# Sigmoid attention and token mixer on one core: order of steps planned anew, all output in 64x64 tiles, exchange and casts on VectorE

## The chip, the core and the metric

The kernel runs on one core of one Trainium2 chip. The metric is the device time of one execution in microseconds (us), lower is better; a kernel's time is the median of its runs. The profile is one further execution; its span counts from the first to the last instruction.

## What is computed

```python
# q, k, v: (8, 12, 448, 64) float32; moe_w_q, moe_w_k: (768, 64); moe_w_out: (768, 768)
scores = q @ k.T / sqrt(64) - log(448)
x = sigmoid(scores) @ v                        # per batch and head
x = x.transpose(0, 2, 1, 3).reshape(8, 448, 768)
wq, wk = x @ moe_w_q, x @ moe_w_k              # (8, 448, 64)
mixed = (wq @ wk.T / sqrt(64)) @ x             # per batch
out = relu(mixed) @ moe_w_out                  # (8, 448, 768)
```

The kernel never forms `wq @ wk.T`: it computes `wk.T @ x` (64 by 768 per batch) and multiplies `wq` with that.

## The kernel before

**Tiling.** Four heads of one batch make a group ("quad" in the code): 24 groups, three to a batch. 448 rows are 64 partitions times 7, so a group's attention is seven steps. A score step (`scores`) is four matmuls of 64x64 tiles, one for each quarter of TensorE, that fill a pair of PSUM banks; one ACT instruction takes the sigmoid of the pair, 128x896, to bf16. A value step (`values`) is four more 64x64 matmuls, which accumulate over the seven steps in another pair of banks; after the seventh, the pair is evicted to `xt`, on DVE as a rule. There are 168 score steps and 168 value steps.

**From the inputs to a group.** Loads are issued on the SP queue into a ring of eight 448 KB buffers (`pump_loads`, order in `ORDER`). Each load of q, k or v is cast to bf16 by POOL, unless `ORDER` marks it: with a dot for DVE, as a capital for ACT (`cast_next`). q and k must then be transposed. Four ways exist, chosen for each group by a letter of the plan:
- "a"/"b" and "q"/"k": transposes on TensorE, in 128x128 or 64x64 blocks, and an eviction from PSUM by DVE;
- "c"/"d": POOL exchanges quadrants of 32 partitions with six copies 32x448 (`arrange`, over the scratch tile `swap`), then DVE transposes 32x32 blocks in two instructions for each of q and k;
- "r"/"s"/"z": no exchange; DVE transposes straight to the exchanged quadrants, two instructions of 128x448 ("r") and four of 32x448 ("s" and "z").

**After a batch's three groups.** `tr_x` transposes `xt` ("X" in 128x128 blocks, "x" in 64x64), `mlp_wqk` makes wq and wk ("W" in 128x128, "w", "l" in 64x64), `mlp_wkn` transposes wk, `mlp_tmp` ("U", "T") makes `wk.T @ x`, `mlp_mix` ("M", "m") multiplies with wq and takes the relu, and the letters "O", "o", "Q", "I", "i" are parts of the output product. For batches in pair `TW` (pairs 1 and 2 of 0 to 3) mixing and output use 64x64 tiles: an output tile is four parts of twelve matmuls in one pair of banks (`out_pair`), and `mlp_mix` writes 256-column halves. For pairs 0 and 3 the output is made in 128x128 tiles of 384 columns (`out_chunk`) or in 64x64 tiles with a sum on DVE (`out_halves`). 64x64 output needs the rows of w_out a second time with the partition halves exchanged: the letter "C" copies one block of `wout16` with two DMAs on SP, six letters in all. w_out itself is loaded and cast by two DMAs from POOL's queue (`load_wout`, when POOL comes to the entries w1 and w4 of `ORDER`).

**What sets the order.** Nothing is scheduled by a library. `PLAN` is a string of 639 letters, worked off from left to right by the last loop; each letter issues one step. An engine's instructions run in the order in which they were issued, and TensorE waits where a step waits. "S" is a score step with its sigmoid, "P", "p", "R" a value step, "1" the next cast of DVE's list, "2" the next of ACT's, "F" a matmul of zeros. `BANKS` names, for every step that opens a PSUM result, the bank or pair of banks (eight in all); a bank is written again when its readers are done. POOL's casts are issued as early as `ready` allows: two buffers each for casted q and k, four for v. From the 45th load on (`LATE`), two loads are let go for each finished output tile, and stand behind that tile's stores on SP.

Score steps are counted below from 0 to 167: group n begins with step 7n.

## Time and profile before

| | |
|---|---|
| median of 3 runs | 183.79 us (182.34 to 184.23) |
| span of the profiled execution | 180.4 us |
| PE, matmuls | busy 170.3 us, 94% of the span |
| ACT | busy 159.0 us, 88% |
| DVE | busy 143.7 us, 80% |
| POOL | busy 122.9 us, 68% |
| DMA | 47.29 MB, mean 262 GB/s |

PE is TensorE's matmuls, PEld its weight loads, DVE VectorE, ACT ScalarE, POOL GpSimd, SP the engine that issues most DMAs. A row of a group gives line, engine, operation, out<-in, shapes and count, then busy us and the mean ns of one, then the idle time in front of them and what ended it. Matmuls overlap, so the mean of one is longer than the time by which it moves the next one on. The share of an engine's busy time is a mean over stretches with different limits, and has to be read stretch by stretch.

### The profile page before, as it was taken

To read this page: it belongs to the slowest core of one execution; us is meant where nothing else is said; L and a number is where in the kernel's file an instruction comes from. 1 tells how busy PE (TensorE), PEld (TensorE's weight loads), DVE (VectorE), ACT (ScalarE), POOL (GpSimd) and SP (SyncE) were. 2 spreads that over 40 slices of the span, in tenths; PEclk is the share of its full clock that TensorE was granted. 3 is DMA by queue.
4 is the path that set the end of the run, shared out by engine and by line. 5 is a ranking of instruction groups with operands and counts; after the bars stand their busy time and mean duration, and the time that the engine had idled before them with its cause. 6 is when DMAs were issued, how large, how long until landed. Compare 5 with 4: busy or idle time off the path is not lost.

```text
span 180.4 us, 7849 instructions
## 1 busy us (share of the span) xinstructions
PE 170.3 (94%) x3412; PEld 114.1 (63%) x3412; DVE 143.7 (80%) x226; ACT 159.0 (88%) x208; POOL 122.9 (68%) x167
## 2 busy tenths in 40 slices
PE   7898899889999999999999999999999999999990
PEld 7444445444675555546667786677888888888660
DVE  3566899998988896989999999978789885868351
ACT  4599999999999999999999999998999989976310
POOL 1076899798999999999999999889978810010000
PEclk9999999999999999999999999999999999999999
DMA  5999999999999989699997999968596432505876
GB/s 169 353 394 346 325 385 376 283 304 366 339 305 358 349 266 299 226 318 349 279 318 277 257 307 329 372 215 272 137 336 166 131 88 48 137 4 123 207 196 174
DMA packets 24914, 47.29 MB, mean 262 GB/s; under 512 B 3888, under 2 KB 18480, under 8 KB 24880
## 3 DMA queue, kind: packets, MB, share of 16 engines
q1 hardware_dynamic: 23600, 44.64, 76.8%
q0 software_dynamic: 800, 1.18, 3.6%
q10 hardware_dynamic: 480, 0.98, 1.5%
q8 instruction: 26, 0.43, 0.9%
q14 instruction: 8, 0.07, 0.1%
HBM read 35.78 MB, written 11.01 MB: 259 GB/s over the span
## 4 chain that ended last, share of the span: by engine, by line
PE 61%; DMA 16%; ACT 7%; POOL 5%; DVE 4%; SPq 3%; issue 2%; POOLq 0%
PE banks L530 15%; PE banks L341 11%; PE banks L319 11%; PE banks L611 9%; DMA k<-in_k_dram 8%; ACT at L324 7%; DMA v<-in_v_dram 5%; DMA w<-in_moe_w_k_dram 4%; PE banks L570 3%; POOL qk L192 2%; PE banks L404 2%; PE banks L416 2%; PE banks L379 2%; PE banks L363 2%; PE banks L484 1%
## 5 line engine op out<-in xcount | busy, mean ns | idle before, releaser
L324 ACT ACTIVATE at<-banks 128x896 bf16<-128x896 f32 x168 | 139.8, 951 | 2.9 <-PE banks L319 2.4
L319 PE MATMUL banks<-qk 64*64 64x448 bf16 x672 | 62.0, 357 | 3.3 <-ACT at L324 2.0
L341 PE MATMUL banks<-at,v 64*64 64x448 bf16 x672 | 47.3, 351 | 0.8 <-ACT at L324 0.7
L319 PEld LDWEIGHTS <-qk 64*64 64x64 bf16 x672 | 25.7, 105 | 21.5 <-issue 13.3
L530 PE MATMUL banks<-wout,mx 64*64 64x384 bf16 x672 | 36.2, 323 | 0.0
L192 POOL CAST qk<-k 128x896 bf16<-128x896 f32 x19 | 22.7, 1196 | 10.1 <-DMA k<-in_k_dram 9.7
L341 PEld LDWEIGHTS <-v 64*64 64x64 bf16 x672 | 23.2, 106 | 8.4 <-issue 1.8
L350 DVE CAST xt<-banks 128x896 bf16<-128x896 f32 x22 | 23.8, 1084 | 2.5 <-PE banks L341 2.0
L530 PEld LDWEIGHTS <-mx 64*64 64x64 bf16 x672 | 22.6, 107 | 4.5 <-issue 0.2
L611 PE MATMUL banks<-wout,mx 128*128 128x384 bf16 (+1 forms) x138 | 24.4, 320 | 0.0
L192 POOL CAST qk<-q 128x896 bf16<-128x896 f32 x18 | 21.5, 1193 | 2.5 <-DVE qk L276 1.0
L471 DVE TENSOR_SCALAR mx<-banks 128x1024 bf16<-128x1024 f32 (+3 forms) x22 | 21.3, 970 | 1.9 <-PE banks L484 0.7
L209 POOL CAST v<-v 128x896 bf16<-128x896 f32 x22 | 20.6, 952 | 1.8 <-DMA v<-in_v_dram 1.3
L611 PEld LDWEIGHTS <-mx 128*128 128x128 bf16 x138 | 12.3, 98 | 9.8 <-issue 3.2
L167 POOL COPY qk<-swap 32x448 uint32<-32x448 uint32 x28 | 16.3, 584 | 1.6
L276 DVE STREAM_TRANSPOSE qk<-qk 128x448 f32<-128x448 f32 x28 | 17.0, 628 | 0.5 <-POOL qk L164 0.4
L161 POOL COPY swap<-qk 32x448 uint32<-32x448 uint32 x28 | 15.6, 556 | 2.5 <-DVE qk L192 0.8
L164 POOL COPY qk<-qk 32x448 uint32<-32x448 uint32 x28 | 15.6, 555 | 1.6
L245 DVE STREAM_TRANSPOSE qk<-qk 32x448 f32<-32x448 f32 x24 | 15.3, 636 | 0.6
L413 POOL COPY wq<-wqk 64x448 bf16<-64x448 bf16 x3 | 1.7, 556 | 15.8 <-DVE wqk L412 15.8
L644 DVE COPY o<-banks 128x384 f32<-128x384 f32 x12 | 6.6, 553 | 5.7 <-PE banks L611 5.3
L392 DVE COPY xn<-banks 128x1024 bf16<-128x1024 bf16 (+1 forms) x14 | 8.8, 625 | 2.8 <-PE banks L379 2.7
(89 smaller groups left out, 203.8 us busy)
## 6 DMA issues: line engine op xcount, KB each, us to landing
q<-in_q_dram SPq DMA_DIRECT2D x24, 448.0 KB, 6.3
v<-in_v_dram SPq DMA_DIRECT2D x24, 448.0 KB, 6.0
k<-in_k_dram SPq DMA_DIRECT2D x23, 448.0 KB, 6.9
out_dram<-o SPq DMA_DIRECT2D x50, 192.0 KB, 4.2
wout<-in_moe_w_out_dram POOLq DMA_DIRECT2D x2, 576.0 KB, 11.6
wout<-wout SPq DMA_DIRECT2D x12, 96.0 KB, 6.4
out_dram<-o ACTq DMA_DIRECT2D x4, 192.0 KB, 3.2
k<-in_k_dram SPq DMA_DIRECT2D x1, 256.0 KB, 4.8
```

Of the source, the lines that this page charges most:

```text
L161: eng.tensor_copy(out=z[lo], in_=w[hi, 0])
L167: eng.tensor_copy(out=w[lo, 1], in_=z[lo])
L192: COPY[e](out=f[:, :, "qk".index(nm)].rearrange("p e i d y -> p e y i d"), in_=ld.pop((nm, n)).rearrange("p (y i e d) -> p e y i d", y=2, ...
L209: COPY[e](out=t16.rearrange("p b i d -> p (b i d)"), in_=ld.pop((nm, n)).rearrange("p b x -> p (b x)"),)
L276: nc.vector.transpose(out=qk[n][:, t].rearrange("p t i n -> p (t i n)").bitcast(F32), in_=w)
L319: nc.tensor.matmul(sc[HALF[h], g, 0:S], qk[n][HALF[g], h, 1, i, :], qk[n][HALF[g], h, 0].rearrange("p i n -> p (i n)"), start=True, stop=True,
L324: inst = nc.scalar.activation(at, sc[:, :, 0:S], ACTF.Sigmoid, bias=attn_bias, scale=attn_scale)
L341: nc.tensor.matmul(ps[HALF[g], h, 0:S], ld["v16", n][HALF[h], g, i, :], ats[n, i][HALF[h], g, :], start=(i == 0), stop=(i == NI - 1),)
L350: read(fb, COPY[eng](out=xt(u, j)[:, :, 0:S], in_=ps[:, :, 0:S]))
L471: inst = nc.vector.tensor_scalar(dst, ps, moe_scale, 0.0, ALU.mult, ALU.max)
L530: nc.tensor.matmul(ps[HALF[x], y, 0:NB], mx[HALF[y], u, b, 64 * (i - 3 * y) : 64 * (i - 3 * y) + 64], wout16[HALF[y], slot(y, b), x * NB : ...
L611: nc.tensor.matmul(ps, mxs[w][:, 2 * S * c + m * P : 2 * S * c + (m + 1) * P], wout16[:, c, w0:w1], start=(c == 0), stop=(c == NC - 1),)
```

## The change

`PLAN`, `BANKS` and `ORDER` are replaced as a whole. By the letters and the instructions that come of them:
- All four pairs of batches are in `TW`: the output is made by `out_pair` alone (28 tiles), mixing in 256-column halves; `out_chunk` and `out_halves` are not used.
- Groups 1, 2, 3 and 6 are transposed on TensorE in 64x64 blocks ("q"/"k"; before: group 1 in 128x128, groups 3 and 6 in 64x64). Groups 4 and 5 have the new letter "v": loads and casts as for "c", but the six exchange copies are issued on DVE, at the place of the letter, in front of the transposes. All other groups, 7 to 23, are exchanged on POOL (17 groups, 14 before). The way "r"/"s"/"z" (six groups before) is not used.
- 21 casts stand on DVE (k1, q1 to q4, k6, q12, k13, k18, q18 and eleven of v; six before), none on ACT (before: one of v and three entries of w).
- `tr_x` uses 128x128 blocks 3 times instead of 10; five matmuls of zeros instead of ten.
- The copies "C" stand together while batch 0 is mixed, between score steps 29 and 36; on SP, one stands behind the load of q8 and the other five, ten DMAs, behind that of k9. Before they stood between steps 35 and 84.
- `LATE` is 46 instead of 44.

```diff
--- before.py
+++ after.py
@@ -65,17 +65,17 @@
     banks16 = banks.rearrange("p b x -> p (b x)").bitcast(BF16).rearrange("p (b x) -> p b x", b=8)
 
     BANKS = (
-        "01 23 45 7 7 67 01 23 5 5 45 67 45 1 01 23 67 5 5 45 3 23 1 01 67 5 45 23 01 67 45 01 45 "
...
+        "01 23 45 7 7 67 01 23 5 5 45 67 01 4 45 23 67 01 23 45 67 01 23 45 67 23 45 01 23 67 45 "
+        "01 45 67 01 45 67 01 45 23 0 45 67 1 23 45 0 67 23 45 1 67 01 45 2 67 01 23 45 67 01 23 "
+        "45 67 23 01 67 23 01 67 23 45 6 23 7 45 01 23 45 23 01 67 45 6 01 67 4 01 23 45 67 23 "
...
     )
     BANKS = BANKS.split()[::-1]
 
@@ -126,23 +126,23 @@
         return xts[u % 2 * NJ + j]
 
 
-    TW = (1, 2,)
+    TW = (0, 1, 2, 3, )
 
 
     PLAN = (
-        "FFSSSFFKSSF11aSSbFFrSFSFSSFSqSPPsPPSPzkPSPSPPPSxSrSsPPPPSPPS"
-        "PSPPPPSSXWzSSwWWSWWXSNSSPPPrSsPPUSPPzSPSPSPCMPPPSPSqkSSMSXSM"
-        "SCcPPPSPPxSPdPSOSwwrSSwwWWxSOSSOsOSNPPSPPzCPSPPSIISISIcPSPdP"
-        "PSPS2SPPOOSxSUSPPSMPPPcSPPSdOwWwSSMWWWoSMPPSPPPP1SSPcdOQSxSO"
-        "OSSNCSOOXcdSSOOSTSPPPSrPPCPSPPCPPSPPPSPSOwowSSSwsOzOxSwwWPSP"
-        "MSPPPPRSScSdXXOXoSMSOoNSMPPSPcPPSPPSUdSOSMOSOMoPSPPcPPSPSdPw"
-        "WXWSMSWWWXSSONOScTSOSOSOOdSPOSrOSPPPGPPSPPPSPPsPSPOSPOSOzSQS"
-        "XPcPPSPPPSPOSOdSOSxOlLlSLlLPSPPPxPP2GSPOOScOmdOSOOSNO1SQSTPP"
-        "PcS1PPSPOPSOSOQSMOSOSOdScOOSdOMSOmOP2PSPPxSPPP12SOSOSOSxOllL"
-        "SllcSLPPPSPPPSPOOdSxSOOSOSOSONQSTPSPPPSPPPSPPPxPPmPPLxLlMlGL"
-        "lOOyOoNIItIiIMimIiMOoOOOoOoOOOOOOOOOoOO"
+        "FFSSSFFKSSF1S11qSkS1SSqPP1RkpSpSRPqSkSSRRRSx1SSvPPSRdSSPPpRp"
+        "RSPPSSXSSWWWSvWWSWXSdPPpCPPSPNPSS1SCUqkSCSCCSMMCSPSpRSMPSpPS"
+        "PRSPPRS1cRSRPWWWSXSSWxWWSdPRSxRcRSPRNSPSUSxSMRdpSpSMSPppPSoS"
+        "OSQcSOOdSoSGoOSoS1QxSOS1OSPRSRpcPdpPSPRpSpxSRPPSQS1oxSOScdOS"
+        "OOS1oSOS1PPPRSpPPlSlllcdSllSOOS1QOSRPSRPpNSpPcdSOoSOSxQtSxSw"
+        "wwwwwGRpSPRNGPRGRSTocdSoSOQSxoSO1SMcOSOpPRSPmRPPQSoSdMQSORPS"
+        "RxpSRPPSQcSQxdSOSO1S1pPpRRSORSoSPQSOSoQcdSxSQ1OcSLLLSLLLSPPR"
+        "SppPPSoSOSdxOSOpSppRSpRNPSwUScSxwwwwwpGpSNppdPGGRuSPQSQSMQSQ"
+        "QcdSQSxOGOS1QSOMSQSOSPpPRScP1doSoRSPOSOSPRpPSPpPcSQSQxSQSdOL"
+        "1SLLLLSLSQocSoSOPSPRPdSPNpPSOSQxSQQSpTSPRSppPPSRPpmPPPplmllm"
+        "lllyyoOxNoOQtOooMQmOMoQOoooOoOOoooOOQOQ"
     )
-    KIND = ["a"] + [t for t in PLAN if t in "qacer"]
+    KIND = ["a"] + [t for t in PLAN if t in "qacerv"]
 
     ld = {}
     SRC = dict(q=q, k=k, v=v)
@@ -152,7 +152,7 @@
     def arrange(n, eng):
 
         arranged.add(n)
-        if KIND[n] in "er":
+        if KIND[n] in "r":
             return
         w = pq[n].rearrange("p e t i d y -> p e (t i d y)").bitcast(U32)
         z = p_one.tile([P, 2 * NI * 32], U32, tag="swap", name="swap")
@@ -168,7 +168,7 @@
 
     def load1(n, nm, eng):
         u, j = quads[n]
-        if KIND[n] in "cer" and nm != "v":
+        if KIND[n] in "crv" and nm != "v":
             t = p_ld.tile([P, 2 * NI * HD], F32, tag="ld", name=nm + "32")
             eng.dma_start(
                 out=t, in_=SRC[nm][u, 4 * j : 4 * j + 4].rearrange("h (p r) d -> (h p) (r d)", r=2 * NI),
@@ -185,7 +185,7 @@
         ld[nm, n] = t
 
     def cast1(n, nm, e):
-        if KIND[n] in "cer" and nm != "v":
+        if KIND[n] in "crv" and nm != "v":
             if n not in pq:
                 pq[n] = p_c16.tile([P, 2, 2, NI, 32, 2], BF16, tag="qk16", name="qk16")
             f = pq[n]
@@ -195,7 +195,10 @@
             )
             ld[nm + "16", n] = f
             if ("q16", n) in ld and ("k16", n) in ld:
-                arrange(n, nc.gpsimd)
+                if KIND[n] == "v":
+                    arranged.add(n)
+                else:
+                    arrange(n, nc.gpsimd)
             return
         if nm == "v":
             t16 = p_v16.tile([P, 2, NI, HD], BF16, tag="v16", name="v16")
@@ -268,7 +271,9 @@
             for e in range(2):
                 nc.vector.transpose(out=qk[n][:, e].rearrange("p t i n -> p (t i n)").bitcast(F32), in_=w[:, e])
             return
-        if kind in "cdef":
+        if kind == "v":
+            arrange(n, nc.vector)
+        if kind in "cdefv":
             assert n in arranged
             w = pq[n].rearrange("p e t i d y -> p e (t i d y)").bitcast(F32)[:, t]
             if t == 0:
@@ -694,10 +699,10 @@
 
 
     ORDER = (
-        ".q1 .k1 k2 q2 q3 v0 w2 k3 v1 k4 q4 v2 w0 k5 q5 w1 v3 W5 v4 q6 k6 w4 k7 v5 q7 v6 q8 k8 k9 "
-        "q9 v7 q10 v8 k10 v9 k11 q11 k12 k13 v10 .q12 q13 v11 v12 v13 q14 k14 k15 q15 v14 q16 k16 "
-        "v15 q17 k17 k18 q18 q19 v16 v17 v18 k19 V19 W3 q20 .q22 q21 k20 W6 k21 .k22 v20 q23 k23 "
-        "v21 .v22 v23 "
+        ".k1 .q1 .q2 k2 .v0 .q3 k3 v1 k4 .q4 v2 k5 w0 q5 q6 v3 .k6 v4 v5 w1 .v6 k7 w4 k8 q7 q8 "
+        "v7 q9 k9 q10 k10 .v8 .v9 .q12 k11 q11 .v10 k12 q13 .k13 .v11 v12 k14 q14 q15 k15 .v13 "
+        "v14 k16 q16 v15 k17 q17 .k18 .q18 v17 .v16 q19 k19 v18 q20 k20 k21 q21 .v19 q22 .v20 "
+        "k22 k23 q23 .v21 v22 v23 "
     )
     BY = {"s": [], "v": []}
     for x in ORDER.split():
@@ -711,7 +716,7 @@
     done = dict.fromkeys("SPqkKxWNUMOCgz", 0)
     used, loaded, cast = set(), set(), set()
 
-    LATE = 44
+    LATE = 46
     ring = [("q", 0), ("k", 0)]
 
     allowed = [2]
@@ -812,7 +817,7 @@
     used |= {("q", 0), ("k", 0)}
     pump()
 
-    ALIKE = dict(a="q", c="q", e="q", r="q", b="k", d="k", f="k", s="k", j="k", h="k", X="x", y="x", Y="x", g="g", z="z", L="W", l="W", T="U", t="U", I="O", i="O", Q="O", G="M", R="P")
+    ALIKE = dict(v="q", a="q", c="q", e="q", r="q", b="k", d="k", f="k", s="k", j="k", h="k", X="x", y="x", Y="x", g="g", z="z", L="W", l="W", T="U", t="U", I="O", i="O", Q="O", G="M", R="P")
     done["q"] = done["k"] = 1
     quads_r = []
 
@@ -843,7 +848,7 @@
             tr(c, kind, t)
             if t in "df":
                 used.add(("q", c))
-            if t not in "cers":
+            if t not in "cersv":
                 used.add((kind, c))
                 pump()
         elif t == "g":
```

18 rows, old and new, of the table BANKS are left out of this document.

## Prediction

> **What bounds the kernel now.** I read the page's head first, then the busy time in stretches, cut where the sigmoids reach a certain number, then the chain of waits. The head has the span:
>
> ```profile
> span 180.4 us, 7849 instructions
> ```
>
> The median of the three runs is 183.79 us, 3.4 more than this span; I add 3.4 to a span to get a time. The next view gives busy us and number of instructions for PE, PEld, DVE, ACT and POOL in each stretch, then clock, DMA share and GB/s:
>
> ```profile
> 0.00:7.00 7.00, 6.01 (x56) 4.79 (x56) 3.05 (x16) 2.51 (x5) 0.70 (x6) 1.00 0.72 222
> 7.00:58.20 51.20, 47.06 (x892) 25.86 (x888) 44.03 (x67) 51.20 (x63) 42.31 (x53) 1.00 1.05 345
> 58.20:90.20 32.00, 31.91 (x512) 17.88 (x508) 27.77 (x42) 31.18 (x42) 30.19 (x41) 1.00 0.91 299
> 90.20:155.60 65.40, 64.77 (x1578) 50.45 (x1571) 55.53 (x78) 63.38 (x81) 49.12 (x68) 1.00 0.74 231
> 155.60:176.00 20.40, 20.40 (x400) 15.13 (x392) 12.79 (x25) 10.69 (x22) 0.56 (x1) 1.00 0.51 129
> ```
>
> Three regimes. From 7 to 58 us ACT is busy 51.20 of 51.20: sigmoids set the pace, and PE is not full. From 58 to 155.6 us PE (31.91 of 32.00, 64.77 of 65.40) and ACT are both full. After that PE alone works. The sigmoids themselves, in the same stretch and over the run:
>
> ```profile
> 7.00:58.20 51.20, 51.20 (x63) 1.00 1.05 345
> ```
> ```profile
> L324 ACT ACTIVATE at<-banks x168: 911/934/1086, 7.0 to 155.6; 128x896 bf16<-128x896 f32 x168
> ```
>
> So one sigmoid costs 51.20/63 = 0.81 us, and in the first regime sigmoid number k (from 0) is due at 7.0 + 0.81k. I write S23 for number 23, which belongs to group 3 (7 a group). The last one starts at 155.6, and the last eviction stands in the chain at
>
> ```profile
> 176.20 0.36 DVE o L633
> ```
>
> which leaves 4.2 us for it and the last store.
>
> **PE's work.** The chain of waits has start and length of each block, start to start where PE is the bound:
>
> ```profile
> 86.89 0.45 PE banks L363 x8
> 87.33 0.49 PE banks L611 x3
> 87.82 0.31 PE banks L319 x4
> 88.13 0.22 PE banks L484 x8
> 88.35 0.19 PE banks L319 x4
> ...
> 94.30 0.49 PE banks L530 x12
> ```
>
> Three 128x128 matmuls (L611) and twelve 64x64 ones (L530) do the same share of the output in the same 0.49 us: 64x64 tiles neither cost nor save streaming. Four score matmuls take 0.19 us behind 64x64 work but 0.31 behind L611: a change of tile shape costs up to 0.12 us. In the order of instructions there are 68 such changes before and 34 after. Those before S63 (35 and 25) lie in the stretch where ACT is the bound. Between S63 and S98 they go from 22 to 2, behind that from 11 to 7.
>
> Transposes of x in eight 128x128 blocks (L363) take 0.45 us. The 64x64 form, by starts in the timeline,
>
> ```profile
> 45.02 0.45 PE L379 MATMUL banks<-ident,xt 64*64 64x64 bf16 x32
> 45.30 0.36 PE L319 MATMUL banks<-qk 64*64 64x448 bf16 x4
> ```
>
> takes 0.28. The wide form goes from 10 to 3 uses. Mixing in 256-column halves is eight matmuls in 0.22 (L484), where the form for batches 0, 1, 6 and 7 had four of 448 columns, 0.19 like the scores: 12 times 0.03, nothing.
>
> I add up each stretch's matmuls by their columns at 448 in 0.19 us (quarter tiles four at a time), and the tile changes at 0.12. S63 to S98: before 27.9 + 2.6 = 30.5 of the 32.0 us, after 31.4 + 0.2 = 31.6, since output steps have been moved forward into this stretch: +1.1. S98 to the last sigmoid: before 63.5 + 1.2 = 64.7 of 65.4, after 61.3 + 0.8 = 62.1: -2.6. After the last sigmoid: 20.5 (for the 20.40) against 18.7: -1.8.
>
> **ACT and the evictions.** These groups carry the prices that follow (busy us, mean ns):
>
> ```profile
> L350 DVE CAST xt<-banks 128x896 bf16<-128x896 f32 x22 | 23.8, 1084 | 2.5 <-PE banks L341 2.0
> ...
> L192 POOL CAST qk<-q 128x896 bf16<-128x896 f32 x18 | 21.5, 1193 | 2.5 <-DVE qk L276 1.0 <-DMA q<-in_q_dram 0.9 <-POOL qk L167 0.4
> ...
> L276 DVE STREAM_TRANSPOSE qk<-qk 128x448 f32<-128x448 f32 x28 | 17.0, 628 | 0.5 <-POOL qk L164 0.4
> ...
> L161 POOL COPY swap<-qk 32x448 uint32<-32x448 uint32 x28 | 15.6, 556 | 2.5 <-DVE qk L192 0.8
> ...
> L541 DVE COPY o<-banks 128x384 f32<-128x384 f32 x4 | 2.2, 557 | 1.2 <-PE banks L530 0.9 <-issue 0.3
> ...
> L469 ACT ACTIVATE mx<-banks 128x512 bf16<-128x512 f32 x2 | 1.2, 600 | 0.5 <-PE banks L484 0.5
> ...
> L788 DVE CAST k<-k 128x512 bf16<-128x512 f32 x1 | 0.4, 427 | 0.4 <-DMA k<-in_k_dram 0.4
> ...
> L788 DVE CAST k<-k 128x384 bf16<-128x384 f32 x1 | 0.4, 360 | 0.1
> ```
>
> ACT gets eight half relus (L469, 0.60) before its last sigmoid instead of two and loses about as many output copies and a cast: I count +1. It falls between S63 and the end of the sigmoids, where PE's work becomes less; with PE, ACT and DVE then all within some per cent of full, I take +0.7 (0 to +1.5). The last store is 192 KB a DMA instead of 96, its eviction 0.56 (L541) instead of 0.36. Median us to landing:
>
> ```profile
> k<-in_k_dram SPq DMA_DIRECT2D x23, 448.0 KB, 6.9
> out_dram<-o SPq DMA_DIRECT2D x50, 192.0 KB, 4.2
> wout<-in_moe_w_out_dram POOLq DMA_DIRECT2D x2, 576.0 KB, 11.6
> ...
> out_dram<-o SPq DMA_DIRECT2D x2, 96.0 KB, 2.5
> ```
>
> That would be +1.9; the 4.2 comes from busier stretches, so I take +0.7.
>
> Without new waits: 180.4 + 1.1 - 2.6 - 1.8 + 0.7 + 0.7 = 178.5, a time of 181.9.
>
> **The new waits.** After the change 21 casts (6 before, 4 of them after the start) and 12 exchange copies run on DVE. None of it is on PE, but DVE takes its work in order, and the evictions that free PSUM banks stand behind. What DVE and POOL do to each other is in the timeline (start, length):
>
> ```profile
> 64.48 1.58 POOL L167 COPY qk<-swap 32x448 uint32<-32x448 uint32 x2
> ...
> 126.56 1.17 POOL L164 COPY qk<-qk 32x448 uint32<-32x448 uint32 x2
> ```
> ```profile
> 64.98 0.68 DVE L192 CAST qk<-q 128x896 bf16<-128x896 f32 x1
> ```
> ```profile
> 142.25 1.06 DVE L209 CAST v<-v 128x896 bf16<-128x896 f32 x1
> ```
> ```profile
> 141.90 2.20 POOL L209 CAST v<-v 128x896 bf16<-128x896 f32 x2
> ```
>
> Two POOL copies take 1.17 us alone and 1.58 when a DVE cast from SBUF to SBUF starts between them: POOL pays 0.4. At 142 us a cast on DVE takes 1.06 instead of some 0.65 because a POOL cast is under way, and the POOL pair takes 2.20. Each holds the other up. [...]
>
> The place where it matters is group 4. Its exchange ("v" in the plan) stands on DVE behind S17, so from about 20.8 us. Behind it stand both transposes of group 4 and then the eviction of group 1's values, whose bank pair is the one S23 writes; S23 is due at 7.0 + 23 x 0.81 = 25.7. A DVE copy of 448 words lies between the two L788 rows: 0.39. Without waits: 20.8 + 6 x 0.39 + 2 x 0.63 + 1.08 = 25.5, just in time. But POOL's timeline there, with nearly the same casts after the change, is
>
> ```profile
> 20.59 0.94 POOL L209 CAST v<-v 128x896 bf16<-128x896 f32 x1
> 22.10 2.18 POOL L760 CAST wqk<-w 64x384 bf16<-64x384 f32 x4 [0.57 <-DMA w<-in_moe_w_k_dram]
> 24.35 1.19 POOL L192 CAST qk<-k 128x896 bf16<-128x896 f32 x1
> 25.44 1.19 POOL L192 CAST qk<-q 128x896 bf16<-128x896 f32 x1
> ```
>
> If each copy waits for one of these: 0.94 + 4 x 0.55 + 1.19 = 4.3 more, and S23 is 4.1 late. Group 5's exchange, behind S26, holds up the eviction of batch 0's wqk, for which PE waits ahead of S30: 0 to 1.2. ACT has no other work there, so this is lost. I take 3.0 of the 0 to 5.3, about half, as POOL also waits for loads.
>
> Late, POOL is the engine with little room: it exchanges 17 groups instead of 14 (six copies of 0.56), and 15 casts on DVE that meet it cost 0.4 each, 6 us. Loads for group 22 are queued on SP behind a store at S137, 17 steps ahead of S154. At 65.4/70 = 0.93 a step that is 15.9 us. They need 6.9 to land, two casts (2.4), the exchange (3.3) and two transposes (1.3), 13.9, and SP waits for the evictions of the stores in front:
>
> ```profile
> SPq L551 <- DVE o L543: 13.2, 4, 4.5
> ```
>
> 13.2 us in 4 waits. I take 1.5 (0 to 4) for this and group 23.
>
> The sum: 178.5 + 3.0 + 1.5 = 183.0, a time of **186.4 us**.
>
> **Rivals.** *The waits do not come* (the copies slip between POOL's instructions, POOL keeps its lead): 181.9, and down to 179.7 where the levelled engines cost nothing, the store lands as now and half of the 1.5 us that PE's sum leaves free between S63 and S98 goes too. It decides at group 4: exchange and transposes done by 24.5, S23 is not late. For it: 25.5 against 25.7 fits, and PE's savings lie where PE is 99% busy. Against it: four rows that show the hold-up.
>
> *The weight copies block the loads.* The twelve copies of wout ("C") stand on SP directly behind the loads up to group 8 and 9, ten in a row. The first waits for POOL's casting DMA, 11.6 us to landing, which POOL issues near 32: SP stands until about 43. v7, q9 and k9 are behind it: landed by 50, casts and exchange 5.7, transposes 1.3: 57, against S63 due at 58.2. One us of room; with the exchanges' hold-ups and ten more issues ahead of q10 and k10 up to 4 us go: 187 to 190. Against it: SP idle lets the weights land sooner.
>
> *The change is neutral*: half of the waits, 183 to 185.5; speaks for it that each wait was priced at half of a wide range.
>
> **Chances.** Under 1% (1.8 us here) I call no change. Forecast, slower by waits on DVE and POOL: 0.42. SP blocked by the weight copies, slower: 0.09. No waits: 0.34, of which 0.07 ends within 1%. Neutral: 0.15. So faster 0.27, same 0.22, slower 0.51. The range: low end 179.7 (the first rival), high end 191.0 (5.3 and 2.7 for the waits instead of 3.0 and 1.5, and the store's 1.9), together 8 in 10.
>
> **What would show it.** Right: six exchange copies on DVE near 21 us that last over 4 us together with gaps to POOL's instructions; a wait of ACT for scores of 1 us or more between 24 and 33; the sigmoids from S63 to the last in about 98 us (97.4 before); PE after the last sigmoid 18.7. POOL copy pairs of 1.6 instead of 1.17 where DVE casts. Wrong: S63 at 58 us (then the waits were nothing), or ACT waiting for PE in 60 to 155 where I see PE relieved, or SP's wait for wout as the longest.

## The result and the profile after

| | median us | runs |
|---|---|---|
| before | 183.06 | 181.49 to 184.23 |
| after | 198.43 | 195.25 to 200.86 |
| ratio | 1.080 | 95% interval 1.064 to 1.096 |

The change costs 8%, where 186.4 us (179.7 to 191.0) were predicted. The ratio is of the faster executions of each kernel, and the profiled execution of the kernel after, 200.86 us, is the slowest of its four.

The head of the page after, then one row of the page before:

```profile
span 199.0 us, 9232 instructions
...
PE 172.2 (87%) x4122; PEld 123.7 (62%) x4123; DVE 146.6 (74%) x216; ACT 160.5 (81%) x207; POOL 121.0 (61%) x169
...
PEclk9996889987999999999879999999999999999998
...
q8 instruction: 32, 0.52, 1.1%
```
```profile
q8 instruction: 26, 0.43, 0.9%
```

PE is less busy (87%, 94% before), it has 1421 instructions more, its clock dips four times, and queue q8 fetches 32 packets, each of 16,384 bytes, instead of 26. The stretches below are cut at the starts of S0, S35, S63, S98 and of the last sigmoid (columns as in the prediction: busy us of PE, PEld, DVE, ACT, POOL, then clock, DMA share, GB/s). Before, the rows that the prediction did not need:

```profile
7.00:35.30 28.30, 25.10 (x432) 12.77 (x425) 23.00 (x36) 28.30 (x36) 21.41 (x24) 1.00 1.05 356
35.30:58.20 22.90, 21.95 (x460) 13.09 (x463) 21.04 (x32) 22.90 (x29) 20.90 (x29) 1.00 1.05 332
...
155.60:180.40 24.80, 20.56 (x400) 15.13 (x392) 13.26 (x26) 10.69 (x22) 0.56 (x1) 1.00 0.53 137
```

After:

```profile
6.70:44.00 37.30, 25.35 (x568) 15.01 (x562) 27.89 (x39) 29.37 (x35) 21.95 (x25) 0.90 0.99 317
44.00:69.00 25.00, 23.44 (x494) 14.74 (x490) 20.01 (x26) 23.74 (x30) 19.63 (x28) 0.94 0.84 284
69.00:109.00 40.00, 34.85 (x878) 25.45 (x874) 29.29 (x45) 33.22 (x46) 29.80 (x43) 0.96 0.72 231
109.00:174.70 65.70, 63.75 (x1612) 48.64 (x1604) 54.69 (x75) 62.14 (x80) 48.35 (x68) 1.00 0.73 224
174.70:199.00 24.30, 19.11 (x554) 15.04 (x544) 11.77 (x19) 9.61 (x18) 0.56 (x1) 0.96 0.49 125
```

The loss has two main places: 9.0 us before S35, where ACT is no longer busy throughout (29.37 of 37.30), and 8.0 us between S63 and S98, where nothing is: PE 34.85, ACT 33.22 of 40.00. From S35 to S63 2.1 us more are lost, behind S98 nothing in sum.

**Between S63 and S98.** PE's timeline (start, length, line, tiles; idle time in front):

```profile
90.81 0.36 PE L535 MATMUL banks<-wout,mx 64*64 64x384 bf16 x4
92.43 1.01 PE L535 MATMUL banks<-wout,mx 64*64 64x384 bf16 x20 [1.26 <-issue]
...
95.67 0.44 PE L384 MATMUL banks<-ident,xt 64*64 64x64 bf16 x26
98.35 0.31 PE L384 MATMUL banks<-ident,xt 64*64 64x64 bf16 x6 [2.24 <-issue]
```

PE stops inside an output part, after 4 of 24 matmuls, and inside a run of transposes, after 26 of 32. The operands of the next matmul are the same tiles; "issue" says that the profile shows no wait. If matmuls and weight loads are counted together from the first record on, both stops are in front of the 193rd of a 256, give or take two (a few records are missing), and so are nine more gaps of 0.3 us or more from start to start. If these are the ends of blocks of 256, the first block has 64 instructions ahead of the first record, which the trace does not show. The longest eight, from the starts in the trace, with the packets of q8:

```
PE goes on at   start to start   line it stands at   last instruction packet landed
16.20           1.81             L346                14.65
22.40           1.70             L384                20.92
64.52           1.11             L535                63.01
79.81           1.29             L324                78.60
92.43           1.58             L535                91.11
98.35           2.43             L384                96.80
121.29          1.28             L535                119.95
163.51          0.86             L409                162.06
```

32 packets of 256 instructions are 8192, against 8245 records of PE. PE goes on 1.2 to 1.6 us after a packet has landed: as if it had waited for its own instructions, which the first experiments test. The eleven pauses sum to 13.3 us.

**Before S35.** The exchange of groups 4 and 5 on DVE, the cast of k6, and what POOL does meanwhile:

```profile
22.67 0.69 DVE L397 COPY xn<-banks 128x1024 bf16<-128x1024 bf16 x1 [2.50 <-PE banks L384]
...
24.06 1.11 DVE L161 COPY swap<-qk 32x448 uint32<-32x448 uint32 x2
25.20 1.20 DVE L164 COPY qk<-qk 32x448 uint32<-32x448 uint32 x2
26.43 2.31 DVE L167 COPY qk<-swap 32x448 uint32<-32x448 uint32 x2
28.77 1.17 DVE L281 STREAM_TRANSPOSE qk<-qk 128x448 f32<-128x448 f32 x2
29.86 2.05 DVE L355 CAST xt<-banks 128x896 bf16<-128x896 f32 x2
...
38.56 3.15 DVE L218 CAST k<-k 128x896 bf16<-128x896 f32 x1
```
```profile
26.21 1.24 POOL L192 CAST qk<-q 128x896 bf16<-128x896 f32 x1
27.38 1.11 POOL L218 CAST q<-q 128x896 bf16<-128x896 f32 x1
...
38.17 0.78 POOL L666 DMA_DIRECT2D wout<-in_moe_w_out_dram  x1
38.95 1.19 POOL L192 CAST qk<-k 128x896 bf16<-128x896 f32 x1
40.05 1.18 POOL L192 CAST qk<-q 128x896 bf16<-128x896 f32 x1
```

Group 4's six copies last 4.7 us, 0.50 to 1.27 each, and each ends 0.24 to 0.25 us behind the end of a POOL cast; group 5's six, from 32.67 on, take 0.38 to 0.39 each, while POOL does nothing (32.20 to 36.46). The evictions of L355 stand behind them. The cast of k6, 0.58 to 0.73 us in eight other kernels, lasts 3.15: it ends 0.5 us behind POOL's second cast (41.23). PE waits for both, and ACT for PE (idle time in brackets):

```profile
30.97 0.38 PE L324 MATMUL banks<-qk 64*64 64x448 bf16 x4 [2.64 <-DVE xt L355]
...
41.77 0.41 PE L232 MATMUL banks<-ident,k 64*64 64x64 bf16 x28 [1.89 <-DVE k L218]
```
```profile
31.40 8.43 ACT L329 ACTIVATE at<-banks 128x896 bf16<-128x896 f32 x10 [1.88 <-PE banks L324]
42.42 3.35 ACT L329 ACTIVATE at<-banks 128x896 bf16<-128x896 f32 x4 [2.59 <-PE banks L324]
```

### The profile page after: what moved, and what is told of

It reads as the page before. It is cut to its first block, busy times and chain, and to the rows that moved or that the text cites. A ratio compares the mean times of both kernels' runs of the same rounds, so it can differ in the third digit from the quotient of the medians.

```text
span 199.0 us, 9232 instructions
## 1 busy us (share of the span) xinstructions
PE 172.2 (87%) x4122; PEld 123.7 (62%) x4123; DVE 146.6 (74%) x216; ACT 160.5 (81%) x207; POOL 121.0 (61%) x169
## 4 chain that ended last, share of the span: by engine, by line
PE 70%; ACT 11%; DVE 10%; issue 5%; ACTq 0%; DVEq 0%
PE banks L535 27%; PE banks L324 14%; PE banks L346 13%; ACT at L329 10%; PE banks L384 3%; PE banks L421 3%; PE banks L409 2%; PE banks L489 2%; PE banks L694 2%; DVE k L218 2%; DVE qk L167 2%; PE banks L450 1%; PE banks L465 1%; DVE qk L281 1%; DVE xt L355 1%
## 5 line engine op out<-in xcount | busy, mean ns | idle before, releaser
L535 PE MATMUL banks<-wout,mx 64*64 64x384 bf16 x1344 | 71.0, 323 | 3.3 <-issue 3.2
L535 PEld LDWEIGHTS <-mx 64*64 64x64 bf16 x1344 | 46.0, 107 | 13.9 <-issue 5.2
L346 PEld LDWEIGHTS <-v 64*64 64x64 bf16 x672 | 25.2, 110 | 10.6 <-issue 4.0
L355 DVE CAST xt<-banks 128x896 bf16<-128x896 f32 x22 | 23.8, 1084 | 6.7 <-PE banks L346 6.2
L548 DVE COPY o<-banks 128x768 f32<-128x768 f32 x20 | 19.1, 954 | 12.1 <-PE banks L535 5.3
L281 DVE STREAM_TRANSPOSE qk<-qk 128x448 f32<-128x448 f32 x38 | 23.2, 627 | 0.1
L476 DVE TENSOR_SCALAR mx<-banks 128x512 bf16<-128x512 f32 (+1 forms) x23 | 20.3, 896 | 3.7 <-PE banks L489 3.7
L212 POOL CAST v<-v 128x896 bf16<-128x896 f32 x13 | 12.4, 963 | 2.4 <-DMA v<-in_v_dram 1.9
L384 PEld LDWEIGHTS <-xt 64*64 64x64 bf16 x672 | 9.4, 109 | 6.2 <-issue 4.2
L384 PE MATMUL banks<-ident,xt 64*64 64x64 bf16 x672 | 9.7, 194 | 3.8 <-issue 3.7
L489 PE MATMUL banks<-wqk,tmp 64*64 64x256 bf16 x96 | 10.1, 284 | 0.6 <-DVE qk L312 0.6
L489 PE MATMUL banks<-wq,tmp 64*64 64x256 bf16 x96 | 9.6, 284 | 0.7 <-ACT mx L474 0.7
```

Of the source, the lines that this page charges most:

```text
L281: nc.vector.transpose(out=qk[n][:, t].rearrange("p t i n -> p (t i n)").bitcast(F32), in_=w)
L346: nc.tensor.matmul(ps[HALF[g], h, 0:S], ld["v16", n][HALF[h], g, i, :], ats[n, i][HALF[h], g, :], start=(i == 0), stop=(i == NI - 1),)
L355: read(fb, COPY[eng](out=xt(u, j)[:, :, 0:S], in_=ps[:, :, 0:S]))
L384: nc.tensor.transpose(ps[HALF[c], g, (2 * m + h) * HD : (2 * m + h + 1) * HD], xt(u, j)[HALF[g], h, (2 * m + c) * HD : (2 * m + c + 1) * H ...
L476: inst = nc.vector.tensor_scalar(dst, ps, moe_scale, 0.0, ALU.mult, ALU.max)
L489: nc.tensor.matmul(ps[HALF[x], y, 256 * z : 256 * z + 256], tmps[u][HALF[y], c * P + 64 * z : c * P + 64 * z + 64], wq[y][HALF[y], 192 * x ...
```

## The experiments

All but fetch_alone in one table: starts in us in the profiled execution; PE instructions are matmuls and weight loads by the plan (the traces hold 8 or 9 fewer); "pauses" are the gaps of 0.3 us and more, from start to start, in front of the 193rd of 256 PE instructions, give or take two. Waits for other engines that happen to stand there are included: mostly short ones, but 4.2 us in hybrid and 3.9 us in hybrid_x are a wait for a copy of wout. phase64 and fetch_alone were run once, the others four times or more; the kernel before, run beside them each time, had medians from 182.31 to 183.99.

| kernel | median | PE instructions | pauses, sum | S35 | S63 | last sigmoid | span |
|---|---|---|---|---|---|---|---|
| before | 183.06 | 6832 | 2.0 | 35.3 | 58.2 | 155.6 | 180.4 |
| after | 198.43 | 8254 | 13.3 | 44.0 | 69.0 | 174.7 | 199.0 |
| phase64 | 197.60 | 8318 | 8.9 | 43.1 | 67.9 | 171.1 | 195.8 |
| x_wide | 196.67 | 7246 | 0.8 | 43.1 | 67.2 | 168.7 | 193.6 |
| tw12 | 197.70 | 7162 | 6.0 | 44.4 | 69.2 | 171.5 | 195.9 |
| exch_pool | 199.35 | 8254 | 12.6 | 42.5 | 65.9 | 172.5 | 196.6 |
| k6_pool | 196.87 | 8254 | 9.4 | 43.8 | 67.5 | 170.5 | 195.3 |
| exch_pool_late | 201.98 | 8254 | 12.2 | 43.6 | 67.5 | 173.4 | 197.8 |
| early_whole | 192.85 | 7918 | 2.1 | 42.9 | 66.3 | 163.8 | 187.9 |
| exch_fix | 199.66 | 8254 | 14.6 | 40.1 | 64.2 | 174.3 | 198.9 |
| mend | 193.86 | 7918 | 9.3 | 40.1 | 64.8 | 167.0 | 191.6 |
| mend64 | 197.75 | 7982 | 11.6 | 40.6 | 64.1 | 170.9 | 195.5 |
| mend_x | 193.44 | 6910 | 0 | 40.5 | 64.5 | 166.5 | 191.8 |
| mend2 | 193.75 | 7918 | 3.3 | 43.9 | 67.4 | 166.3 | 190.9 |
| mend2_x | 194.44 | 7390 | 1.5 | 43.0 | 67.0 | 168.4 | 193.2 |
| before_tw123 | 184.84 | 7228 | 2.8 | 35.3 | 58.2 | 156.3 | 182.1 |
| hybrid | 209.53 | 8068 | 12.4 | 36.2 | 78.0 | 186.5 | 211.0 |
| hybrid_x | 208.63 | 7636 | 4.9 | 35.0 | 75.4 | 181.5 | 206.5 |
| hybrid2 | 192.98 | 7588 | 4.7 | 34.9 | 59.4 | 166.9 | 191.4 |

### Are the pauses a matter of instructions?

**phase64** shifts the count by 64, with the same work:

```diff
-    for _ in range(32):
-        nc.tensor.matmul(banks[:, 6, 0:P], zeros[:, 0:P], zeros[:, 0:P], start=True, stop=True)
+    for _ in range(64):
+        nc.tensor.matmul(banks[:, 6, 0:64], zeros[:, 0:P], zeros[:, 0:64], start=True, stop=True)
```


> 64 warm-up matmuls of 64 columns instead of 32 of 128: the same streaming time, 32 more matmuls and 32 more weight loads ahead of all other work on PE. In the kernel after, PE stands still for 0.4 to 2.4 us at places that are all a multiple of 256 instructions apart (counted over matmuls and weight loads), whatever stands there. Theory F (PE waits for its own instructions, which come in blocks of 16 KB, 256 of them): the stalls stand again at position 192 of each 256 by count, so at other lines, 64 instructions earlier in the work; their sum stays between 7 and 15 us; time within 3% of the kernel after (192 to 204). Rival (the stalls belong to the work: PSUM banks or buffers not free): they stay at the same steps of the work (the values after S13, the x transposes of groups 0 and 13, the output pairs), 64 positions later by count.

The sum and the time are in the expected ranges. Nine of its ten gaps are again in front of the 193rd of 256, give or take two (the tenth, 0.7 us at 8 us, is a wait for DVE), and so at other steps of the work: the longest of after, inside the x transposes at 98 us, is gone, and one of 1.79 us stands at 131 us, where after has none over 0.3. They belong to the count, not to the work.

**fetch_alone** measures the cost by itself, in a kernel of its own:

```diff
+    stream(1024, 384, 0)
+    stream(1024, 64, 2)
...
+            nc.sync.dma_start(
+                out=t,
+                in_=src[n % 24 // 3, 0:4].rearrange("(g h) (p i) d -> (h p) g (i d)", g=2, i=7),
+            )
+    stream(1024, 384, 4)
+    stream(1024, 64, 4)
```


> The disputed cost by itself; nothing of the reference is computed, the output is zeros. PE runs 4096 matmuls of 64x64 weights without any wait on another engine: 1024 with 384 columns, 1024 with 64 columns, then both again while SP loads 72 times 448 KB (as q, k, v are loaded) into SBUF. Each stretch of 1024 matmuls is 2048 instructions, 8 blocks of 256. By the kernel after, 128 matmuls of 384 columns stream in 5.1 us and 128 of 64 columns in 1.9 us. Theory F: without loads a block of 64 columns takes not 1.9 but some 3 us (the fetch by itself: request to landing, and 1.2 to 1.5 us from the landing to the first instruction), and one of 384 columns 5.1; with loads both become 5.5 to 7 us, with a pause of 1 us or more once per 256 instructions. Rival (PE's instructions arrive far enough ahead, the stalls were waits on other engines): 1.9 and 5.1 in both halves, no pause.

PE's timeline, without loads up to 75 us and with loads behind that:

```profile
57.96 1.92 PE L56 MATMUL banks<-zeros 64*64 64x64 bf16 x128 [1.80 <-issue]
61.69 1.92 PE L56 MATMUL banks<-zeros 64*64 64x64 bf16 x128 [1.80 <-issue]
...
102.21 5.39 PE L56 MATMUL banks<-zeros 64*64 64x384 bf16 x128 [1.08 <-issue]
108.40 5.39 PE L56 MATMUL banks<-zeros 64*64 64x384 bf16 x128 [0.80 <-issue]
...
134.28 1.92 PE L56 MATMUL banks<-zeros 64*64 64x64 bf16 x128 [4.68 <-issue]
140.75 1.92 PE L56 MATMUL banks<-zeros 64*64 64x64 bf16 x128 [4.55 <-issue]
```

A block of 128 matmuls and 128 weight loads starts every 3.5 to 3.7 us without loads (DMA share 0.02) once that has settled, and every 6.2 to 6.5 us with loads that keep the DMA engines full (1.04), whether it streams for 1.9 us, at half clock, or for 5.4, at full clock. So this is the price that the ledger lacked: 256 PE instructions take at least 3.5 to 6.5 us in this kernel, by what the DMA engines have to do. The count of 256 agrees with q8's packets, 32 of 16,384 bytes for 8245 records of PE; in the kernel after the pauses sum to 13.3 us.

### Fewer PE instructions

**x_wide** makes all transposes of x in 128x128 ("x" to "X", "y" to "Y", the first bank of the pair); one line of the plan of many:

```diff
...
-        "PRSPPRS1cRSRPWWWSXSSWxWWSdPRSxRcRSPRNSPSUSxSMRdpSpSMSPppPSoS"
+        "PRSPPRS1cRSRPWWWSXSSWXWWSdPRSXRcRSPRNSPSUSXSMRdpSpSMSPppPSoS"
...
```


> All 24 transposes of x in 128x128 instead of 21 of them in 64x64, nothing else: 1008 PE instructions fewer of 8254. Theory F (instruction fetch): fewer blocks of 256 go by in under 6 us, the long stalls inside the x transposes (1.5 us at 21, 2.2 us at 96) go and others get shorter; stall sum from some 11 us to 4 to 8, time 4 to 8 us less than the kernel after (190 to 195). Rival (the ledger of the prediction: each change of tile shape 0.12 us, a wide transpose 0.17 us more than one in 64x64): 0.4 us more for each of the transposes that stand on PE's path, 0 to 8 us slower than the kernel after (198 to 206).

**tw12** makes the output of batches 0, 1, 6 and 7 in 128x128 as before:

```diff
-    TW = (0, 1, 2, 3, )
+    TW = (1, 2)
```


> Output of the first and the last quarter (batches 0, 1, 6, 7) in 128x128 tiles as in the kernel before, the rest as after: 1092 PE instructions fewer, 14 more evictions of 384 columns for 14 fewer of 768, four stores of 96 KB late. Theory F: the four or five stalls of 0.4 to 1.6 us that stand in the outputs of batches 0 and 1 (64 to 93 us) shrink to under 0.3; time 3 to 7 us less than the kernel after (191 to 196). Rival (the ledger of the prediction): 20 changes of tile shape more between S63 and S98 at 0.12 us and 1.8 us more behind the last sigmoid, 3 to 5 us slower than the kernel after (199 to 204).

In both the pauses shrink as expected (to 0.8 in one; to none between S63 and S98 in the other), but the time does not fall as expected, by 3 to 8 us; it hardly moves: 1.0745 (1.0652 to 1.0838) and 1.0838 (1.0733 to 1.0943) of the kernel before. S63 to S98 took 35.6 and 36.8 us instead of 40.0, against 32.0 before. Wide transposes and tile changes (some 30 between S63 and S91 in tw12, none after, by the trace) take back what the pauses gave: this fits the prices of the prediction (0.45 us for a wide transpose against 0.28, up to 0.12 for a tile change) and was not tried by itself. The small tiles save the tile changes that the ledger counted, and pay for them in instructions.

**early_whole** takes only the early q and k transposes of four groups back to 128x128:

```diff
-        "FFSSSFFKSSF1S11qSkS1SSqPP1RkpSpSRPqSkSSRRRSx1SSvPPSRdSSPPpRp"
-        "RSPPSSXSSWWWSvWWSWXSdPPpCPPSPNPSS1SCUqkSCSCCSMMCSPSpRSMPSpPS"
+        "FFSSSFFKSSF1S11aSbS1SSaPP1RbpSpSRPaSbSSRRRSx1SSvPPSRdSSPPpRp"
+        "RSPPSSXSSWWWSvWWSWXSdPPpCPPSPNPSS1SCUabSCSCCSMMCSPSpRSMPSpPS"
```


> The q and k transposes of groups 1, 2, 3 and 6 on TensorE in 128x128 (7 a tensor) instead of 64x64 (28), each evicted by itself: 336 PE instructions fewer, nearly all before 20 us, and four evictions more on DVE of 0.6 us for four fewer of 1.1. Theory F: the two stalls of 1.5 us at 14.7 and 20.9 (blocks that went by in under 5 us) shrink under 0.5, the half clock that follows them goes, group 3 starts at 25 to 26 instead of 27.8; time 1 to 3 us under the kernel after. Rival (these stalls are waits for values' banks and loads): they stay, no gain.

192.85 us at the median, 189.71 to 195.81: 5.6 less than after, where 1 to 3 were expected. No pause is left before S35, group 3 starts at 24.5 us, and 2.1 us of pauses are left in all. Behind S63 PE has the same instructions in the same order as after:

```profile
6.30:42.90 36.60, 27.02 (x400) 14.06 (x394) 29.87 (x44) 29.34 (x36) 21.71 (x26) 0.95 1.04 330
42.90:66.30 23.40, 22.20 (x486) 14.22 (x489) 19.41 (x26) 23.28 (x31) 18.67 (x28) 1.00 0.90 298
66.30:99.80 33.50, 32.67 (x878) 24.95 (x873) 28.75 (x45) 32.79 (x45) 29.33 (x42) 1.00 0.85 275
99.80:163.80 64.00, 63.30 (x1612) 47.76 (x1608) 54.14 (x76) 61.93 (x79) 49.39 (x69) 1.00 0.75 230
163.80:187.90 24.10, 18.95 (x554) 15.61 (x546) 11.81 (x19) 9.64 (x18) 0.56 (x1) 0.94 0.51 127
```

From S63 to the end the same 878, 1612 and 554 matmuls take 121.6 us here, 130.0 after, 130.7 in exch_pool and 127.8 in k6_pool. It is the fastest execution of a kernel that scatters by 6 us, and how many pauses the other three have is not on record. That block ends now fall on other work, and that other loads meet their fetches, would explain the fewer pauses and was not tried.

**mend64** repeats the shift on a later version (mend, below), to see whether pauses of this size are time:

> The mended kernel with 64 warm-up matmuls of 64 columns instead of 32 of 128 (same streaming time, 64 instructions more ahead of everything): only the place of the block boundaries in the work moves. Theory F: the sum of the stalls depends on which work falls into a block, so it changes by some us in either direction (1 to 8 us in sum), and the time with it by about the same; stalls at position 192 of 256. Rival (stalls of this size are not the time): the same time within 0.5% with another sum of stalls.

11.6 us of pauses instead of 9.3, and 197.75 us instead of 193.86: a shift of the count by 64 instructions is worth 2% by itself.

The traces answer the question more widely. Ten kernels have the same 6036 PE instructions behind S63, in the same order but for neighbours. Their pauses behind S63 and the time from S63 to the end, in us:

| | early_whole | mend2 | k6_pool | phase64 | mend | after | exch_pool_late | exch_pool | mend64 | exch_fix |
|---|---|---|---|---|---|---|---|---|---|---|
| pauses behind S63 | 1.8 | 2.9 | 7.2 | 7.3 | 7.4 | 8.7 | 10.1 | 10.1 | 10.9 | 13.2 |
| S63 to the end | 121.7 | 123.5 | 127.8 | 127.9 | 126.7 | 130.0 | 130.3 | 130.6 | 131.3 | 134.7 |

They lie on a line, each within 1.1 us: 119.9 us without pauses and 1.08 us more for each us of pauses. So behind S63 a pause costs its length, and without pauses the new order would take 2.3 us less there than the kernel before (122.2).

### The early part

**exch_pool**: the exchange of groups 4 and 5 on POOL ("v" to "c", twice).

```diff
-        "FFSSSFFKSSF1S11qSkS1SSqPP1RkpSpSRPqSkSSRRRSx1SSvPPSRdSSPPpRp"
+        "FFSSSFFKSSF1S11qSkS1SSqPP1RkpSpSRPqSkSSRRRSx1SScPPSRdSSPPpRp"
...
```


> The exchange of groups 4 and 5 on POOL, as for the later groups, instead of on DVE; nothing else. Theory D (the step of the prediction: the exchange fills DVE, whose copies meet POOL's casts, and the evictions behind it come late): the waits of ACT of 1.9 us at 29.5 and of 2.6 us at 40 go or fall under 1 us each, 3 to 5 us less than the kernel after (193 to 196). Rival (POOL has no room for 12 copies of 0.56 us there: the exchange stands behind casts and the casting DMA, groups 4 to 7 come later): 0 to 5 us slower than the kernel after.

**k6_pool**: the cast of k6 on POOL (its "1" and its dot taken out).

```diff
-        "...XSdPPpCPPSPNPSS1SCUqkSCSCCSMMC..."
+        "...XSdPPpCPPSPNPSSSCUqkSCSCCSMMC..."
-        "... q5 q6 v3 .k6 v4 v5 ..."
+        "... q5 q6 v3 k6 v4 v5 ..."
```


> One of the 21 casts that the change put on DVE, that of k of group 6, goes back to POOL; nothing else. In the kernel after this cast lasts 3.15 us on DVE (38.6 to 41.7) instead of 0.63, with four instructions of POOL under way, and group 6's transposes, the scores and ACT (2.6 us) wait for it. Theory D (DVE's copies meet POOL's): the wait of 2.6 us goes, group 5 starts 2 to 3 us earlier, and the kernel is 1.5 to 3 us faster than after. Rival (POOL has no room): the cast comes after POOL's other work, q6's transposes wait as long, no gain.

Neither gained what was expected: 199.35 and 196.87 us. With the exchange on POOL, DVE waits 4.5 us for it, in front of the same evictions. With k6 on POOL its wait is gone, but group 4 starts at 37.7 us instead of 35.5, and group 5 as late as after.

**exch_pool_late** and **exch_fix**: the transposes of both groups behind the evictions; then also v3 and v4 ahead of q5 and q6.

```diff
-        "...x1SSvPPSRdSSPPpRpRSPPSSXSSWWWSvWWSWXSdPPpCPPSPNPSS1SC..."
+        "...x1SSPPSRSSPPpRpRSPPcSSXdSSWWWSWWSWXSPPpCPPSPNcPSdS1SC..."
-        "... w0 q5 q6 v3 .k6 v4 v5 ..."
+        "... w0 v3 q5 v4 q6 .k6 v5 ..."
```


> Groups 4 and 5 exchanged on POOL, and their transposes on DVE moved behind the evictions of the values of groups 1 and 2 (group 4) and of batch 0's wqk and wkn (group 5), which stood behind them. With the exchange on POOL but the transposes in front, ACT still waited 2.2 us at 29 and 1.1 at 37 us. Theory P (what counts is the place in DVE's queue, ahead of evictions, whichever engine exchanges): the waits of ACT between 26 and 40 us fall under 1 us together, group 5 starts at 39 to 41 us instead of 42.5 (exchange on POOL) and 44.0 (after); time 2 to 4 us under the exchange on POOL alone. Rival (POOL's exchange itself is late): the transposes end as late as before (30 and 36 us), group 4's scores wait for them, no gain.

Group 4 now starts 5.6 us behind group 3 (7.7 after), as expected. Group 5 does not follow, for a reason that neither theory had. PE in this run:

```profile
36.17 1.17 PE L346 MATMUL banks<-at,v 64*64 64x448 bf16 x20 [3.32 <-POOL v L212]
```

v3's cast stands on POOL behind group 5's exchange.

> As the run with the exchange of groups 4 and 5 on POOL and their transposes behind the evictions, and the casts of v3 and v4 ahead of q5 and q6 in POOL's and SP's order, since PE waited 3.3 us there for v3, which stood behind group 5's exchange. Theory P (the early loss is a matter of places in DVE's and POOL's queues): the 3.3 us go, group 5 starts at 39 to 40.5 us (44.0 after, 43.6 in that run); the rest as there, with its fetch stalls; time 194 to 197. Rival (POOL has too much to do before 40 us): q5's exchange comes later by the two casts, group 5 at 43 or later, no gain.

Group 5 at 40.1 us, 3.5 earlier, as expected; the time is not (199.66, from 195.29 to 200.93), since this order has the most pauses of all, 14.6 us.

**mend** adds the wide early transposes to exch_fix; **mend_x** also makes all x transposes wide; **mend2** puts group 5's exchange back on DVE, behind the evictions of wqk and wkn; **mend2_x** has the middle x transposes wide in addition.

> As the run before in this call, and the q and k transposes of groups 1, 2, 3 and 6 in 128x128. If the loss of the change is the two causes together, PE's instruction blocks and the places of group 4's and 5's exchange, and nothing else: group 3 at 24.5 to 25 us as with the wide early transposes alone, group 4 at 30 to 31, group 5 at 36 to 37 (35.3 before); fetch stalls of 2 to 6 us in sum; span 181 to 185, time 184 to 188. Rival (a third cause, so far hidden, for example the loads that come later or the late plan of S91 to S97): group 5 over 39, or S63 to the last sigmoid over 101 us though the stalls are under 3; time over 190.

> The run before in this call with all x transposes in 128x128 as well: 1008 PE instructions fewer again, 6910 in all (6832 in the kernel before). Theory F: no stall over 0.5 us is left; S63 to the last sigmoid as in the run with only the x transposes wide, 101.5 us, since what the stalls give back is paid for by tile changes and wide transposes (0.17 us each); time 1 to 4 us more than the run before in this call, unless that one has stalls of over 4 us, then the same. Rival: the fewer instructions still gain, time below it by 2 us or more.

> As the mended kernel (early q and k transposes in 128x128, group 4 exchanged on POOL and transposed behind the evictions), but group 5's exchange on DVE, behind the evictions of wqk and wkn of batch 0, and q6 cast on POOL ahead of v4. Theory P: q6 is cast by 32 us, group 5 starts at 36 to 38 us instead of 40.1; S0 to S35 30 to 31.5 us. Rival (a third cause keeps group 5 late): 39.5 or later. The fetch pauses behind that depend on how the loads fall: 2 to 9 us in sum, time 186 to 192.

> The run before in this call, with the x transposes of the groups that end between S35 and S98 in 128x128 (528 PE instructions fewer). Theory F: pauses of 0.4 us and more sum to under 3 us, S35 to S98 as with all x transposes wide, 58 to 60 us (61.1 with the wide early transposes alone had 56.9), S98 to the end as with the early transposes alone; time 185 to 190. Rival (the pauses depend on the loads more than on the number of instructions): pauses stay over 4 us in sum.

mend has group 4 at 31.1 us, near the expected 30 to 31, but group 5 at 40.1: now q6's cast is late on POOL.

```profile
37.19 0.56 PE L240 MATMUL banks<-ident,q 128*128 128x128 bf16 x7 [1.01 <-POOL q L218]
```

mend2, which was to cure that, did not: 43.9. DVE takes 3.7 us for the copies (35.72 to 39.44) while POOL casts. mend and early_whole have one PE program and differ by the places of DVE's and POOL's work alone: 9.3 us of pauses against 2.1. mend_x has none and the same time as mend, as expected. mend2_x has pauses under 3 us (1.5), as expected, but 194.44 us instead of 185 to 190; mend and mend2 are over their ranges too (193.86 where 184 to 188 were expected, 193.75 where 186 to 192 were).

**hybrid**, **hybrid_x** and **hybrid2** undo the early part: up to S63 the kernel before, then the kernel after. In the first two the first output is already in 64x64, for which all six copies "C" stand before S45; hybrid2 keeps the output of batches 0 and 1 in 128x128. hybrid_x has nine x transposes behind S63 in 128x128.

```diff
-        "FFSSSFFKSSF1S11qSkS1SSqPP1RkpSpSRPqSkSSRRRSx1SSvPPSRdSSPPpRp"
...
+        "FFSSSFFKSSF11aSSbFFrSFSFSSFSqSPPsPPSPzkPSPSPPPSxSrSsPPPPSPPS"
...
```


> Undoing one part of the change: up to S63 the order, loads and casts of the kernel before (group 1 in wide transposes, groups 2, 4, 5 transposed by DVE's quadrants without an exchange, two casts on DVE), with the first two output chunks already in 64x64 and three copies of wout, and three tensors of mx moved to that end; from S63 on the order of the kernel after. 8068 PE instructions. If the early loss is the early part of the change (S0 to S35 28.3 us before, 37.3 after): S35 at 35 to 36 us, S63 at 58.5 to 61 (69.0 after, 58.2 before). Behind S63 the pauses for instructions stay, 3 to 10 us in sum: S63 to the last sigmoid 99 to 106 us; time 185 to 192. Rival (the late part loses more when the early part is quicker, since loads and POOL are then behind): S63 to the last sigmoid over 106 us, time over 193.

> The run before in this call with the nine x transposes between S63 and about S105 in 128x128 (432 PE instructions fewer): fewer blocks that are fetched too late where the loads keep the DMA engines full. Pauses of 0.4 us and more under 4 us in sum, 2 to 5 us of it gained back less 1.5 (wide transposes at 0.17 us) and up to 1 for tile changes: 183 to 189, 0 to 3 us under the run before. Rival: the pauses move to other blocks and nothing is gained.

Both took over 208 us, where 185 to 192 and 183 to 189 were expected, by a wait that their own order makes. The chain of waits of hybrid_x:

```profile
44.66 9.99 DMA q<-in_q_dram
...
54.73 0.47 SPq L868
...
55.24 5.53 DMA wout<-wout
...
60.82 2.13 PE banks L534 x22
```

The copies of wout stand on SP behind loads that wait for a free buffer, and ACT waited 15.2 us. But S49 is at 46.3 us (46.6 before, 56.1 after).

> Up to S63 the kernel before (its first two output chunks in 128x128, no copies of wout earlier than there; three tensors of mx and three copies of wout added at S62 to S64), from there the order of the kernel after; output of batches 0 and 1 in 128x128, of the others in 64x64. The two hybrids before it had S49 at 46.3 and 47.5 us (46.6 before, 56.1 after), and then PE waited 15 us for a copy of wout that stood on SP behind loads; here no output needs those copies that early. 7588 PE instructions. If the early part is worth some 9 to 10 us and nothing else was lost in the hybrids but that wait: S63 at 58 to 60 us, S63 to the last sigmoid 98 to 103 (97.4 before, 105.7 after), time 183 to 189. Rival (with the early part undone the loads and casts of the later order come too late, as the waits at 75 to 90 us of the hybrids may say): S63 to S91 over 30 us, time over 192.

```profile
6.30:34.90 28.60, 25.31 (x431) 12.67 (x425) 23.24 (x36) 28.51 (x35) 21.39 (x25) 1.00 1.05 359
34.90:59.40 24.50, 21.48 (x458) 12.28 (x457) 21.16 (x32) 23.02 (x29) 21.93 (x30) 1.00 1.05 327
59.40:101.80 42.40, 39.64 (x706) 20.84 (x706) 29.24 (x47) 36.49 (x49) 28.48 (x42) 0.92 0.78 246
```

S0 to S63 takes 53.1 us (62.3 after, 51.2 before): the early part of the change, with the pauses in it, costs 9 us. Not all of it is gained, since 42.4 us go by from S63 to S98 (40.0 after), where the two orders meet; three tensors of mx and an output tile have to be made up there, and the clock is 0.92, and which of them costs how much was not tried. It was expected at 183 to 189 us and took 192.98.

### The part that should gain

**before_tw123**: the kernel before with the last two batches' output in 64x64 as well.

```diff
-    TW = (1, 2,)
+    TW = (1, 2, 3)
-        "lOOyOoNIItIiIMimIiMOoOOOoOoOOOOOOOOOoOO"
+        "lOOyOoNOOtOoOMOmOOMOOOoOOOOOOOoOOOOOOOQ"
```


> The kernel before with one part of the change alone: the output of the last two batches in 64x64 tiles (396 PE instructions more, all late). The ledger of the prediction: 1.8 us less behind the last sigmoid and 0.6 less ahead of it, 0.7 more for the larger last store: 1.0 to 2.4 us faster than the kernel before. Theory F says the same, since the DMA engines have no loads then and a block's fetch takes under 4 us: no pause over 0.5 us behind S130. Rival (64x64 output costs more than it saves, by evictions of 768 columns or by pauses): the same as before or slower.

1.012 (1.005 to 1.019) of the kernel before: if anything slower, where 1.0 to 2.4 us were to be gained. ACT behind its last sigmoid:

```profile
173.12 0.80 ACT L543 COPY o<-banks 128x768 f32<-128x768 f32 x1 [3.06 <-DMA out_dram<-o]
177.13 0.48 ACT L541 COPY o<-banks 128x384 f32<-128x384 f32 x1 [3.22 <-PE banks L530]
```

In this order an eviction waits 3.06 us for an output buffer whose store has not ended, and there is a pause of 1.0 us at 127.7. No version that was run beats the kernel before.

## Why the prediction was wrong

**The ledger of PE, "Without new waits ... 178.5".** This is the step that failed. It adds up columns and tile changes and holds 1421 further PE instructions for free. So it forecast 1.9 us less behind S63 (1.1 - 2.6 - 1.8 + 0.7 + 0.7), where the kernel after takes 7.8 more. Where the blocks come in time it is right, by the line of the ten kernels (2.3 less without pauses) and part by part: by early_whole's windows S63 to S98 takes 1.5 us more than before (said: 1.1 more), S98 to the last sigmoid 1.4 less (said: 2.6 less on PE, 0.7 of it given back to ACT), the rest 0.7 less (said: 1.8 less, 0.7 given back by the store). In the kernel after the same instructions take 8.4 us longer than in early_whole, with 7 us more of pauses. The prediction's own mark for "wrong", ACT waiting for PE between 60 and 155 us, is what came.

**The waits before S35, "taken 3.0 of the 0 to 5.3".** The mechanism was right, the size was not. The six copies of group 4 last 4.7 us with POOL's casts between them, as said, but that is 2.4 more than six of 0.39, where 4.3 was said: a wait for a whole POOL instruction no copy shows (0.1 to 0.9 us lost each, beside casts of 0.55 to 1.24). ACT waits 1.88 us for the evictions behind them; the copies start at 24.1 us, though, not at 20.8, since DVE waits 2.5 us for transposes of x that stand at a pause. But it took the second hold-up, behind group 5's exchange, for 0 to 1.2 us; there the cast of k6 stands, 3.15 us long, and ACT waits 2.59. early_whole, which has no pause there, needs 60.0 us from S0 to S63 against 51.2 before: 8.8 us in place of 3.0, of which 3.6 fall between S21 and S28 (predicted: 4.1 at most) and 3.5 between S28 and S35 (predicted: 1.2 at most). exch_pool, k6_pool and the mended kernels show why moving single pieces saved little: whichever engine makes the exchange, something behind it in the same queue (evictions, v3, q6, k6) is needed at once. hybrid2, which has the old early part, shows that the 9 us (pauses included) belong to that part as a whole; how they divide among exchange, casts and transposes no run shows.

**The sum.** 183.0 predicted, 8.4 for instructions behind S63, 2.3 for those before (62.3 less 60.0), 5.8 more for the early waits: 199.5 against a span of 199.0; what is left is the 1.5 for POOL that did not come, 1.3 by which early_whole misses the ledger behind S63, and starts of S0. The terms are taken from the runs that they explain, so that the sum closes proves nothing, and they are single executions: the medians of after and early_whole, 198.43 and 192.85, differ by 5.6 us, where the two spans differ by 11.1. That "slower" came true is right for the early part and luck for the rest, where a gain was forecast.

**The late POOL chain, 1.5.** Not seen: group 22 to 23 takes 6.4 us in both kernels.

**SP and the copies of wout.** The ten DMAs behind k9 held SP for 10.6 us, from 41.9 to 52.5, but no group came late by more than 1.3 us there; not tried by itself in the kernel after. In the hybrids the same queue cost 15 us.

**The other rivals.** "No waits" and "neutral" fell with the two steps above.

What stays open: how much of the loss before S63 is the half clock (below), which no run separated from the pauses. From S63 to the last sigmoid only after and exch_fix of the ten kernels have a dip of the clock, and they lie 0.7 and 0.6 us above the line: the half clock is a small part there. Open is also why one execution of the same kernel is 5 us slower than another. That the fetches meet other packets in each would explain it, and was not shown.
